# Streaming attention and a mixture of four experts on one core: a new order of the first loads, the second weight of expert 0 in two halves, and refitted constants of the planner

## The chip, the core and the metric

The kernel runs on one core of a Trainium2 chip. The metric is the device time of one execution in microseconds (us). The core has a matrix engine (TensorE, PE in the profile, with its weight loads as PEld), VectorE (DVE), ScalarE (ACT), GpSimd (POOL) and SyncE (SP), which run side by side and wait for each other by semaphores. Transfers go through DMA queues. POOL issues the loads that convert float32 to bfloat16. SP issues transposes, gates and stores.

## The reference

Inputs are q, k and v of shape (4, 8, 768, 64): batch, heads, positions, head dimension. A query sees the keys of the last 128 positions and the first 4 positions ("sinks"). The attention output is laid out as 3072 rows of 512 and goes through four experts, whose results are summed with weights:

```python
keep = is_sink | in_window                     # n_sink 4, window 128
a = softmax(where(keep, q @ k.T / 8, -1e9))
x = (a @ v).transpose(0, 2, 1, 3).reshape(3072, 512)
p = domain_probs / (domain_probs.sum(-1, keepdims=True) + 1e-09)
for e in range(4):
    h = np.maximum(x @ w1[e], 0.0)             # w1[e]: 512 x 1024
    out += p[:, e:e + 1] * (h @ w2[e])         # w2[e]: 1024 x 512
```

The output is float32, 3072 x 512.

## The kernel before

The whole program is unrolled. While it is emitted, a **planner** in the kernel file keeps a clock for each engine (`t["pe"]`, `t["act"]`, `t["dve"]`, `t["pool"]`, `t["sp"]`, and `t["sw"]` for the queue of POOL's loads) and adds a cost for each instruction that it emits. These clocks exist only while the program is made: on the chip each engine runs its instructions in the order in which they were emitted, and waits where a semaphore says so. So every constant of the planner acts on the program only through the order of the instructions, and through which buffer an instruction uses.

**Units of work.** A batch has three groups of 256 rows, here called pairs: (batch, pair). A *unit* is (batch, pair, expert): the hidden block `H` of 256 rows by 1024. It is made in one of three ways.

- Plain: products `hps` of 128x256 (L1134), for the units ahead of `START`.
- Fast: seven products in place of eight, on forms of w1 and of x that VectorE adds beforehand (L1224).
- Turning: the same seven products, P1 to P7, with 512 columns each, two matmuls to a product (L1336). Their result has rows and columns exchanged. It is gated into two row buffers (tiles `row0`, `row1`, later also `rest` and others) on ScalarE or VectorE, and two DMA transposes on SP (`H<-row`, L1317) bring it into `H`. `TURNED_UNITS` says which units are of this kind, 26 before.

In a turning unit the partial result of P5 is copied into the second row buffer by ScalarE (L1390), VectorE adds the bank of P1 and P6 to it, and P7 and P3 go on from that sum:

```python
def keep(engine):                       # after P5
    nc.scalar.copy(out=c5, in_=y)       # c5: the second row buffer as float32
    u["both"](act(n))
def both(ready):
    def run(engine):
        nc.vector.tensor_add(tiles["V"], c5, tiles["X"])
        at["P7"] = at["P3"] = dve(n)
```

A unit of this kind may be opened when two row buffers will be free soon; a transpose puts its buffer back with the time at which it is planned to be done:

```python
def halves(self):
    return sum(x[0] <= t["pe"] + REST for x in self.resting)
```

**Second products.** For the first two pairs the products with w2 are plain: `second` (L1597), eight matmuls of 512 columns for an expert and 128 rows into one bank `acc`. For the rest they are seven products of 256 columns on forms (`product`, L1511), after VectorE has made sums of `H` (L1451).

**Attention.** For each batch: q and k are loaded as rows (`qkn`, L267, key `n<block>` in the new list) and transposed, on TensorE for the first batch and by SP's DMA (`qkT<-qkn`, L276) later. Then come scores (`sps`, L720), exponentials on ScalarE, masks on VectorE, the product with v and the sinks (`od`, L783 and L790), a reciprocal and a scaling into `onat`, and a transpose into `xT`: on TensorE (`tx`, L854) or by SP's DMA (`xT<-onat`, L807).

**Loop.** At each step the planner lists what may come next on TensorE with the time at which it would be ready and a rank: an attention step, a step of an open unit or a new unit (`first`), a `second`, or a `product`. It emits the one of lowest rank that is ready. `DUE`, `LOW_SECOND`, `OPEN`, `STEP0`, `LOW_PRODUCT` and `HIGH_PRODUCT` are ranks. `SHARE_OF`, `LEAD`, `MIX`, `OVER`, `ALONE`, `BEHIND`, `HOLDS`, `SOON` and `REST` are thresholds. `GATE`, `GATE0`, `SCALED`, `FORM` and `TOKEN` are slacks, by which work for the other engines may be put off. Where nothing is ready in the first 20 us, products without a use (`idle_products`, L596) keep TensorE at work.

**Loads.** The rows of batch 0, w1 of expert 0 in quarters (L349), w2 of expert 0 (L359) and then the other weights are issued by POOL in a list written out by hand. `lands` estimates when each has landed. From the third batch on, a small copy on POOL (`held`, L212) stands in front of each load of q, k and v: it reads a tile that was written lately, so that the load is not issued before.

Of the kernel before, what the change touches and what calls it, by code (L numbers as in the profile page):

```python
# [16 lines left out]
def kernel(  # L17
# [20 lines left out]
    P = 128  # L38
# [24 lines left out]
    TURNED_UNITS = (0, 0, 0, 0, 1, 0, 0, 1, 0, 1, 0, 0, 0, 1, 1, 1, 1, 1, 1, 1, 1, 1, 1, 1, 1, 1, 1, 1, 1, 1, 1, 1, 1, 1, 1, 1)  # L63
    EXPERTS = {(1, 0): (0, 1, 2, 3), (1, 1): (2, 0, 3, 1), (1, 2): (1, 2, 3, 0), (2, 2): (0, 1, 3, 2), (3, 1): (3, 1, 0, 2), (3, 2): (1, 0, 3, 2), (2, 0): (1, 3, 0, 2), (0, 2): (2, 1, 3, 0), (3, 0): (2, 3, 0, 1), (2, 1): (3, 0, 1, 2), (0, 1): (2, 1, 3, 0)}
# [29 lines left out]
    SPACE = 1000  # L94
    GATE_LANDS = 2500
    WIDE = 2
    OPEN = 1.9
    SOON = 35000
# [7 lines left out]
    HOLDS = 3  # L106
# [3 lines left out]
    OVER = 6  # L110
    ALONE = 2.4
    BEHIND = 3900
# [10 lines left out]
    t = {"pe": 1200.0, "act": 0.0, "dve": 0.0, "pool": 1280.0, "sp": 800.0, "sw": 6500.0, "hw": 0.0}  # L123
# [87 lines left out]
    def hold():  # L211
        nc.gpsimd.tensor_copy(out=held, in_=mark[1])  # L212
        pool(2, mark[0])
    ROW = {64: 12.8, 128: 22.6, 256: 41.7, 512: 79.8, 1024: 156.2}
# [142 lines left out]
    def load_w2(e):  # L357
        w2_sb[e] = wpool.tile([P, NFB, Dout], BF16, name=f"w2_{e}", tag=f"w2_{e}")
        nc.gpsimd.dma_start(out=w2_sb[e], in_=moe_w2[e].rearrange("(fb p) d -> p fb d", p=P))  # L359
        lands(("w2", e), F, Dout)  # L360
# [163 lines left out]
    t["sw"] += 500  # L524
    for tb in (2, 3):
        load_nat(0, tb)
    load_v(0, (2, 3))
    load_w1(0, 4, [0])
    load_w1(0, 4, [1])
    load_w1(0, 4, [2])  # L530
    load_w1(0, 4, [3])
# [1291 lines left out]
```

## Time and profile before

| what | value |
|---|---|
| median of 3 runs | 353.14 us (352.71 to 353.69) |
| profiled execution | 352.58 us |
| its span | 350.9 us |
| mean granted clock of TensorE | 0.999 |
| TensorE busy | 345.4 us, 3470 matmuls |
| VectorE busy | 275.8 us |
| ScalarE busy | 215.3 us |
| GpSimd busy | 79.8 us |
| moved by DMA | 47.95 MB, mean 137 GB/s |

The span runs from the first to the last recorded instruction of the profiled execution, and the execution's own time is 1.7 us longer. The runs without profile differ by up to 1.0 us. Matmuls are pipelined, and their ends in the profile are modelled, so that the busy time counts overlaps; the distance from one start to the next tells what a matmul takes. In a timeline a row gives start, duration, engine, line, operation, tiles and count, and in brackets how long the engine was idle ahead of it and what released it. In a list of waits a row gives who waited at which line, for whom, the sum, the count and the longest.

### The profile page before, as it was taken

To read this page: it belongs to the slowest core of one execution; us is meant where nothing else is said; L and a number is where in the kernel's file an instruction comes from. 1 tells how busy PE (TensorE), PEld (TensorE's weight loads), DVE (VectorE), ACT (ScalarE), POOL (GpSimd) and SP (SyncE) were. 2 spreads that over 40 slices of the span, in tenths; PEclk is the share of its full clock that TensorE was granted. 3 is DMA by queue.
4 is the path that set the end of the run, shared out by engine and by line. 5 is a ranking of instruction groups with operands and counts; after the bars stand their busy time and mean duration, and the time that the engine had idled before them with its cause. 6 is when DMAs were issued, how large, how long until landed. Compare 5 with 4: busy or idle time off the path is not lost.

```text
span 350.9 us, 8955 instructions
## 1 busy us (share of the span) xinstructions
PE 345.4 (98%) x3470; PEld 256.2 (73%) x3470; DVE 275.8 (79%) x661; ACT 215.3 (61%) x491; POOL 79.8 (23%) x125
## 2 busy tenths in 40 slices
PE   8999999999999999999999999999999999999996
PEld 4685769756798988786997756856856666666785
DVE  5893999988999998899599779579769594785740
ACT  4865714437656576658545589389588666757411
POOL 8946114430542550800244100000000000000000
PEclk9999999999999999999999999999999999999999
DMA  9999999999996999995799976437336829244421
GB/s 177 178 187 194 220 206 173 176 161 160 172 113 78 167 165 164 158 115 64 99 152 183 141 141 146 91 91 138 73 102 140 153 60 182 60 113 128 92 91 62
DMA packets 173606, 47.95 MB, mean 137 GB/s; under 512 B 158084, under 2 KB 169572, under 8 KB 173564
## 3 DMA queue, kind: packets, MB, share of 16 engines
q0 software_dynamic: 79104, 17.31, 56.7%
q1 hardware_dynamic: 93404, 29.55, 44.8%
q8 instruction: 27, 0.44, 0.5%
q10 hardware_dynamic: 1056, 0.52, 0.5%
q14 instruction: 15, 0.12, 0.1%
HBM read 37.61 MB, written 6.34 MB: 125 GB/s over the span
## 4 chain that ended last, share of the span: by engine, by line
PE 94%; DVE 3%; DMA 1%; ACT 1%; issue 1%; DVEq 0%; ACTq 0%
PE acc L1511 34%; PE cps L1336 22%; PE cps L1224 12%; PE acc L1597 8%; PE hps L1134 7%; PE sps L720 3%; PE od L790 3%; PE acc L596 2%; DMA H<-row 1%; PE od L783 1%; DVE aT L758 1%; PE tx L854 1%; DVE onat L820 0%; PE tr L617 0%; PE sinks L681 0%
## 5 line engine op out<-in xcount | busy, mean ns | idle before, releaser
L1511 PEld LDWEIGHTS <-H 128*128 128x128 bf16 x708 | 66.4, 98 | 20.7 <-issue 1.9
L1511 PE MATMUL acc<-w,H 128*128 128x256 bf16 x420 | 57.4, 273 | 0.0
L748 ACT ACTIVATE aT<-sps 128x512 bf16<-128x512 f32 (+1 forms) x96 | 47.0, 573 | 5.4 <-PE sps L720 5.1
L1354 ACT ACTIVATE cps<-cps 128x512 f32<-128x512 f32 x51 | 29.6, 587 | 20.5 <-PE cps L1336 19.6
L1511 PEld LDWEIGHTS <-S 128*128 128x128 bf16 x320 | 30.6, 98 | 9.4 <-issue 0.6
L1134 PE MATMUL hps<-xT,w 128*128 128x256 bf16 x256 | 32.1, 273 | 0.1
L1336 PE MATMUL cps<-w,T 128*128 128x512 bf16 x104 | 30.9, 379 | 0.3 <-DVE cps L1384 0.3
L835 ACT ACTIVATE onat<-od,R 128x64 bf16<-128x64 f32 x108 | 25.0, 325 | 10.1 <-DVE R L817 9.9
L1336 PE MATMUL cps<-vf,T 128*128 128x512 bf16 x104 | 30.6, 379 | 0.0
L1336 PE MATMUL cps<-w,xT 128*128 128x512 bf16 x104 | 30.3, 379 | 0.0
L1597 PE MATMUL acc<-w,H 128*128 128x512 bf16 x128 | 29.9, 379 | 0.0
L1224 PEld LDWEIGHTS <-w 128*128 128x128 bf16 x448 | 28.2, 98 | 2.1
L1511 PE MATMUL acc<-wf,H 128*128 128x256 bf16 (+1 forms) x216 | 29.7, 271 | 0.0
L1336 PEld LDWEIGHTS <-T 128*128 128x128 bf16 x208 | 19.6, 98 | 11.1 <-issue 0.8
L1377 ACT COPY cps<-cps 128x512 f32<-128x512 f32 x26 | 15.0, 578 | 20.6 <-PE cps L1336 18.7
L1134 PEld LDWEIGHTS <-w 128*128 128x128 bf16 x256 | 24.1, 98 | 4.3 <-issue 0.5
L1572 ACT COPY osb<-acc 128x256 f32<-128x256 f32 x35 | 13.4, 382 | 21.3 <-PE acc L1511 19.9
L740 DVE TENSOR_TENSOR aT<-aT,masks 128x1024 bf16<-128x1024 bf16 (+1 forms) x36 | 22.7, 640 | 3.1 <-ACT aT L748 2.8
L336 POOL DMA_DIRECT2D vx<-in_v_dram x24 | 21.4, 897 | 16.2 <-PE acc L1597 4.8
L1257 DVE SCALAR_TENSOR_TENSOR H<-cps,gates 128x512 bf16<-128x512 f32 x36 | 24.0, 677 | 0.2 <-DMA gates<-gate_rows 0.2
L267 POOL DMA_DIRECT2D qkn<-in_q_dram x22 | 19.4, 882 | 13.5 <-DMA qkT<-qkn 5.4
L267 POOL DMA_DIRECT2D qkn<-in_k_dram x22 | 20.0, 911 | 7.7 <-DMA w<-in_moe_w_dram 6.6
(154 smaller groups left out, 696.7 us busy)
## 6 DMA issues: line engine op xcount, KB each, us to landing
w<-in_moe_w_dram POOLq DMA_DIRECT2D x6, 1024.0 KB, 18.2
out_dram<-osb SPq DMA_DIRECT2D x17, 256.0 KB
vx<-in_v_dram POOLq DMA_DIRECT2D x24, 128.0 KB, 5.8
qkn<-in_q_dram POOLq DMA_DIRECT2D x22, 128.0 KB, 7.3
qkn<-in_k_dram POOLq DMA_DIRECT2D x22, 128.0 KB, 7.2
gates<-gate_rows SPq DMA_DIRECT2D x14, 128.0 KB
w<-in_moe_w_dram POOLq DMA_DIRECT2D x4, 256.0 KB, 6.7
w<-in_moe_w_dram POOLq DMA_DIRECT2D x2, 512.0 KB, 11.7
```

The costliest lines, as they stand in the source:

```text
L267: nc.gpsimd.dma_start(out=nat[b, tb][:, i], in_=(q, k)[i][b, :, tb * P:(tb + 1) * P, :].rearrange("h p d -> p h d"),)
L336: nc.gpsimd.dma_start(out=vx[tb][:, :, 0:D], in_=v[b, :, tb * P:(tb + 1) * P, :].rearrange("h p d -> p h d"),)
L740: nc.vector.tensor_mul(x, x, m[:, None, :].to_broadcast([P, 2 if g == 0 else 4, w if g == 0 else 2 * P]))
L748: nc.scalar.activation(out=a[:, ph], in_=sps[ph][:, 0:w], func=AF.Exp, scale=scale)
L835: nc.scalar.mul(o[:, qi, hp, ph * D:(ph + 1) * D], od[:, qi, ph, 0:D], R[:, qi, ph])
L1134: nc.tensor.matmul(h[:, i].rearrange("p (q n) -> p q n", q=2), lhsT=w1_sb[e][:, db, fb * P:(fb + 1) * P], rhs=xT[b, g][:, :, db], start=(i ...
L1224: nc.tensor.matmul(y[:, f], lhsT=A[:, d, f * P:(f + 1) * P], rhs=T[:, d], start=(m in ("P1", "P5") and f == 0 and d == 0), stop=(d == 1), ...
L1257: nc.vector.scalar_tensor_tensor(out=dst, in0=src, scalar=0.0, in1=gate, op0=ALU.max, op1=ALU.mult)
L1336: nc.tensor.matmul(y.rearrange("p f n -> p (f n)"), lhsT=T[:, d], rhs=A[:, d], start=(m in ("P1", "P5") and d == 0), stop=(d == 1), skip_g ...
L1354: nc.scalar.activation(out=src, in_=src, func=AF.Relu)
L1511: nc.tensor.matmul(y, lhsT=self.operand(b, g, e, m)[:, f], rhs=forms[e][m][:, f, cs], start=(k == 0 and f == 0 and m in (("P1", "P5", "P2" ...
L1597: nc.tensor.matmul(op, lhsT=H[:, fb // QF, fb % QF, s], rhs=w2_sb[e][:, fb, :], start=(fb == 0), stop=(fb == NFB - 1),)
```

## The change

1. The first loads are issued in an order that is given as a list. Before: n2 n3 v2 v3, the four quarters a0 to a3 of w1 of expert 0, then its whole w2, n4 n5 v4 v5, the halves b0 b1 of w1 of expert 1, w2 of expert 1, w1 and w2 of expert 2. After: n2 v2 n3 v3 a0 to a3 s0, then n4 s1 v5 n5 b0 v4 b1 t1 c t2, where s0 and s1 are the halves of w2 of expert 0, t1 and t2 the w2 of experts 1 and 2, and c is w1 of expert 2.
2. The second products of expert 0 are split in the same way: for a pair the first four matmuls of both 128-row blocks, each into a bank of its own, and the last four of both as two further steps.
3. The estimates of when loads land are refitted (`LANDED`, `LATER`, `ROW[256]`, the start of `t["sw"]`).
4. Most other constants of the planner have new values, with the order of experts for each pair (`EXPERTS`) and the choice of turning units (27 in place of 26) among them.
5. Values need both of their v blocks by the estimates; `held` copies one float32 where it copied two bfloat16; idle products are not emitted while both banks are taken; weight forms may be made from a planned 41 us on (`SOON2`).

Which units are plain and which of seven products (`START`) is as before. In the order of instructions of the changed kernel, the matmuls are those of before, except that 56 of 128 columns become 14 of 512, one of 512 columns is added to fill a bank that was never written, three idle products of 256 columns are missing, and there are three more runs of score products between others.

```diff
-    TURNED_UNITS = (0, 0, 0, 0, 1, 0, 0, 1, 0, 1, 0, 0, 0, 1, ...)
+    TURNED_UNITS = (0, 0, 1, 0, 0, 1, 0, 1, 0, 1, 0, 0, 1, 1, 1, 1, 1, 1, 0, 1, ...)
-    EXPERTS = {(1, 0): (0, 1, 2, 3), (1, 1): (2, 0, 3, 1), ...
+    EXPERTS = {(1, 0): (1, 3, 2, 0), (1, 1): (1, 0, 3, 2), ...
-    MIX = 9
-    SHARE_OF = (1.1, 0.94, 0.98)
-    LEAD = (0.995, 0.985)
-    DUE = 2.0
+    MIX = 4
+    SHARE_OF = (1.07, 0.94, 0.96)
+    LEAD = (1.03, 0.94)
+    DUE = 1.2
-    LOW_SECOND = 2.4
-    HIGH_PRODUCT = 2.0
+    LOW_SECOND = 3.2
+    HIGH_PRODUCT = 1.8
-    GATE = 700
-    GATE0 = 1200
-    FORM = 2500
-    TOKEN = 4250
-    MARGIN = 2400
+    GATE = 100
+    GATE0 = 1100
+    FORM = 7000
+    TOKEN = 4000
+    MARGIN = 2700
-    STEP0 = 0.16
+    STEP0 = 0.3
-    REST = 1500
+    REST = 5000
-    SCALED = 1500
+    SCALED = 500
+    LANDED = 1100
+    W2PARTS = 2
+    ORDER = ('n2', 'v2', 'n3', 'v3', 'a0', 'a1', 'a2', 'a3', 's0', 'n4', 's1', 'v5', 'n5', 'b0', 'v4', 'b1', 't1', 'c', 't2')
+    HEAD = 10
+    SOON2 = 41000
+    LATER = {("w2", 1): 800, ("w1", 2): 850, ("w2", 2): 700, ("w1", 1, 0): 300}
-    OPEN = 1.9
-    SOON = 35000
+    OPEN = 1.6
+    SOON = 22000
-    HOLDS = 3
+    HOLDS = 1
-    OVER = 6
-    ALONE = 2.4
-    BEHIND = 3900
+    OVER = 2
+    ALONE = 2.3
+    BEHIND = 4200
...
-    t = {..., "sw": 6500.0, ...}
+    t = {..., "sw": 5700.0, ...}
...
-        nc.gpsimd.tensor_copy(out=held, in_=mark[1])
+        nc.gpsimd.tensor_copy(out=held.bitcast(FP32), in_=mark[1].bitcast(FP32))
...
+        t["sw"] += LATER.get(key, LATER.get(key[:2], 0.0))
         at = max(t["sw"], issued + 800)
         t["sw"] = at + rows * ROW[cols] / 16
-        landed[key] = t["sw"] + 900
+        landed[key] = t["sw"] + LANDED
...
-    def load_w2(e):
-        w2_sb[e] = wpool.tile([P, NFB, Dout], BF16, name=f"w2_{e}", tag=f"w2_{e}")
-        nc.gpsimd.dma_start(out=w2_sb[e], in_=moe_w2[e].rearrange("(fb p) d -> p fb d", p=P))
-        lands(("w2", e), F, Dout)
+    def load_w2(e, parts=1, which=None):
+        ...
+        for i in which or range(parts):
+            nc.gpsimd.dma_start(
+                out=w2_sb[e][:, i * n:(i + 1) * n],
+                in_=moe_w2[e][i * n * P:(i + 1) * n * P].rearrange("(fb p) d -> p fb d", p=P),
+            )
+            lands(("w2", e, i) if i < parts - 1 else ("w2", e), F // parts, Dout)
...
-            ((weight_form, e) for e in range(E) if ahead and form_due(e)), None)
+            ((weight_form, e) for e in range(E) if (ahead or t["pe"] > SOON2) and form_due(e)), None)
...
-    for tb in (2, 3):
-        load_nat(0, tb)
-    load_v(0, (2, 3))
-    load_w1(0, 4, [0])
     ...
-    load_w2(0)
+    for i in ORDER[:HEAD]:
+        items[i][0](*items[i][1:])
...
-                    self.second += [(g, s, e) for s in range(2)]
+                    n = W2PARTS if e == 0 else 1
+                    self.second += [(g, s, e, i, n) for i in range(n) for s in range(2)]
...
-            for fb in range(NFB):
+            for fb in range(i * NFB // n, (i + 1) * NFB // n):
...
-        if soonest < 20000 and soonest > now + 220:
+        if soonest < 20000 and soonest > now + 220 and min(acc_free) < 1e11:
             idle_products(acc[1], 1, G)
```

More of the change, by code (lines that the diff above doesn't have):

```diff
@@ L1580, in second_ready @@
                 return 1e12
-            g, s, e = self.second[0]
-            return max(acc_free[self.turn % 2], landed.get(("w2", e), 1e12), self.H_at.get((0, g, e), 1e12))
+            g, s, e, i, n = self.second[0]
+            free = 0.0 if i else acc_free[self.turn % 2]
+            return max(free, landed.get(("w2", e, i) if i < n - 1 else ("w2", e), 1e12), self.H_at.get((0, g, e), 1e12))
         def emit_second(self):
             ready = self.second_ready()
-            g, s, e = self.second.pop(0)
+            g, s, e, i, n = self.second.pop(0)
             if g not in out_sb:
@@ L1600, in emit_second @@
                 )
-            end = pe(NFB * Dout, ready, n=NFB)
+            end = pe(NFB * Dout // n, ready, n=NFB // n)
             acc_free[bank] = 1e12
+            self.done += NFB * Dout // n
+            self.since = 0
+            if i < n - 1:
+                return
             sc = scale_t[:, 2 * g + s, e:e + 1]
@@ L1618, in emit_second @@
             later("dve" if e else "act", end, 400, run)
-            self.since = 0
-            self.done += NFB * Dout
             if s == 1:
@@ L1658 @@
     asked = []
[L1659 to L1661 removed]
+    loads, turns = [items[i] for i in ORDER[HEAD:]], []
     def nat_loads(b, tbs):
```

40 lines of the change are left out of this document (20 added, 20 removed).

## Prediction

> **What bounds the kernel now.** I read the page first, for the span, the engines' busy time and the chain that ended last.
>
> ```profile
> span 350.9 us, 8955 instructions
> PE 345.4 (98%) x3470; PEld 256.2 (73%) x3470; DVE 275.8 (79%) x661; ACT 215.3 (61%) x491; POOL 79.8 (23%) x125
> PE 94%; DVE 3%; DMA 1%; ACT 1%; issue 1%; DVEq 0%; ACTq 0%
> ```
>
> TensorE is busy in 98% of the span and is 94% of the chain. So the time is TensorE's work at its own rate, and a change of order can only remove or add holes between products. Next I read the waits of TensorE, which list the holes, and a table by stretches of time, to see whether the middle has room left (columns: stretch, us, then PE, PEld, DVE, ACT and POOL busy with counts, granted clock, DMA share, GB/s).
>
> ```profile
> PE acc L596 <- DVE lent L506: 1.4, 1, 1.4
> PE cps L1336 <- DVE cps L1384: 0.3, 1, 0.3
> PE tx L854 <- DVE onat L820: 0.2, 1, 0.2
> ...
> 175.00:200.00 25.00, 25.00 (x314) 21.19 (x312) 23.34 (x56) 12.52 (x37) 8.80 (x15) 1.00 1.47 164
> ```
>
> After the start there is one named hole of 0.3 us and one of 0.2 us. In the middle TensorE is full. There is little left to gain, and any new hole shows at its full length. The one hole is the most useful place of the trace, so I read its timeline.
>
> ```profile
> 156.50 0.59 PE L1336 MATMUL cps<-w,xT 128*128 128x512 bf16 x2
> 156.93 0.59 PE L1336 MATMUL cps<-vf,T 128*128 128x512 bf16 x2
> 157.36 0.60 PE L1511 MATMUL acc<-w,H 128*128 128x256 bf16 x4
> 157.79 0.59 PE L1336 MATMUL cps<-vf,T 128*128 128x512 bf16 x2
> ...
> 159.02 0.60 PE L1511 MATMUL acc<-w,H 128*128 128x256 bf16 x4
> 159.91 0.59 PE L1336 MATMUL cps<-w,T 128*128 128x512 bf16 x2 [0.29 <-DVE cps L1384]
> 160.34 0.59 PE L1336 MATMUL cps<-vf,xT 128*128 128x512 bf16 x2
> 160.86 0.40 PE L720 MATMUL sps<-qkT 64*128 64x128 bf16 x6
> 161.19 0.61 PE L1511 MATMUL acc<-w,H 128*128 128x256 bf16 x4
> ```
>
> Starts give the prices, since the modelled ends overlap. Two products of 512 columns take 0.43 us (156.50 to 156.93), four of 256 take 0.43 us (157.36 to 157.79, 0.109 each), and 128 columns take 0.055. At 159.02 four products of 256 columns should have ended at 159.46, and the next starts at 159.91: the hole costs 0.45 us. Entering a run of scores costs 0.09 us more than its products (160.34 to 160.86 is 0.52 for two of 512).
>
> ```profile
> 154.62 1.79 SPq L1317 DMA_TRANSPOSE H<-row  x1
> 158.54 0.59 ACT L1390 COPY row<-cps 128x512 f32<-128x512 f32 x1 [0.84 <-DMA H<-row]
> 159.16 0.70 DVE L1384 TENSOR_TENSOR cps<-row,cps 128x512 f32<-128x512 f32 x1 [0.72 <-ACT row L1390]
> ```
>
> This is why it is there. A turning unit (seven products P1 to P7 that leave a transposed hidden block in two `row` buffers) copies its P5 result into a row buffer on ScalarE, VectorE adds it, and P7 needs the sum. ScalarE waited 0.84 us because the transpose that empties this buffer for the unit before, issued at 154.62, had not landed until 158.54: 3.92 us from issue to release. From the copy's start to P7's start are 1.37 us.
>
> **The row buffers (REST 1500 to 5000).** REST is how far ahead of a buffer's planned release a turning unit may be opened. In the changed program's order one unit is opened much sooner behind its predecessor than any now: batch 2, pair 0, expert 3 takes both row buffers right after expert 0 of that pair. Its ScalarE copy to `row0` (L1399, once L1390) waits for the transpose of `row0` that ends a run of five on SP: q/k block 4 of batch 3, attention output, q/k block 5, `row1`, `row0`. SP issues them in order, and the attention output is ready only after a reciprocal and four ScalarE scalings.
>
> ```profile
> 160.63 0.18 DVE L817 RECIPROCAL R<-od 128x4 f32<-128x4 f32 x1
> 160.84 0.93 ACT L835 ACTIVATE onat<-od,R 128x64 bf16<-128x64 f32 x4 [0.24 <-DVE R L817]
> ...
> 184.18 9.03 SPq L276 DMA_TRANSPOSE qkT<-qkn  x3
> 193.30 1.26 SPq L807 DMA_TRANSPOSE xT<-onat  x1
> 194.65 2.81 SPq L1317 DMA_TRANSPOSE H<-row  x2
> ...
> 219.36 1.26 SPq L1317 DMA_TRANSPOSE H<-rest  x1
> 222.33 0.37 ACT L1572 COPY osb<-acc 128x256 f32<-128x256 f32 x1 [1.38 <-DMA H<-rest]
> ```
>
> I count from the last attention-output product. Reciprocal and scalings take 1.14 us (160.63 to 161.77), with the hand-over from TensorE some 1.4. Three issues on SP follow before that of `row0` (output, q/k, `row1`), at 1.35 each (193.30 to 194.65): 4.0. From issue to release I have 2.97 us (219.36 to 222.33) and 3.92 us (above). Then 1.37 to P7. In all 9.7 to 10.7 us. The changed order gives TensorE in that time 4 score products (0.22), P4 (0.43), sixteen of 256 (1.74), 8 score products (0.44), eight of 256 (0.87), P1 and P5 (0.87), eight of 256 (0.87), P6 and P2 (0.87), eight of 256 (0.87): 7.2, with two entries into scores 7.4. The rest, 2.3 to 3.3 us, is a hole in front of P7: nothing behind it on TensorE may pass. SP's q/k transpose can itself wait for its rows: the three from 184.18 took 9.03 where three at 1.35 take 4.05, so 1.7 each more, which would make up to 5. If it misses everything, or the transposes are issued sooner than I count, it is nothing. I take 3.6: the middle of 2.3 to 3.3, and half of 1.7. P3 and P4 queue behind P7, and the two row transposes of this unit come as much later; their reader, the second products of that pair, lies several us behind.
>
> **The first loads and the halves of w2.** In front of the first w2 the same rows and w1 quarters stand in POOL's queue as before, only n3 and v2 change places, so its start there is unchanged.
>
> ```profile
> 9.51 3.00 POOL L349 DMA_DIRECT2D w<-in_moe_w_dram  x4
> 12.44 0.95 POOL L359 DMA_DIRECT2D w<-in_moe_w_dram  x1
> ...
> w<-in_moe_w_dram POOLq DMA_DIRECT2D x1, 1024.0 KB, 12.7
> w<-in_moe_w_dram POOLq DMA_DIRECT2D x1, 256.0 KB, 7.9
> ...
> 21.73 3.87 PE L1134 MATMUL hps<-xT,w 128*128 128x256 bf16 x32
> 25.43 5.34 PE L1597 MATMUL acc<-w,H 128*128 128x512 bf16 x24
> ```
>
> The whole w2 of expert 0 is issued at 12.44 and lands 12.7 later, at 25.1. The last w1 quarter is issued 3/4 into the run of four that ended at 12.44, at 11.7, and lands at 19.6. So w2 has the queue for 5.5 us and its first half would land at 19.6 + 2.8 = 22.4. The first product of w2 stood at 25.43, where 32 products from 21.73 end at 25.22: a wait of 0.2, which goes. In the changed order it stands 32 products (3.5), three idle ones (0.33) and two small transposes (0.1) sooner: 21.5. It then waits 0.9 for the first half, and no idle products are planned for it. Net +0.7; at the least −0.2 (it lands sooner than half of it), at the most +2 if n4, which now stands between the halves, delays the second.
>
> The Trainium skill, page "DMA: Bandwidth & Descriptors", section "Anatomy of one DMA — SWDGE (gpsimd) path", gives a DMA of GpSimd's queue a fixed part of about 2.0 us beside its bytes, mostly in the completion, which speaks against halves: by it alone, and if transfers did not overlap, the sum would be 2 us higher. The row of w2 (5.5 us behind four quarters that are themselves queued) leaves no 2 us per transfer on top of the bytes, so I add none.
>
> **Small terms.** 27 units turn in place of 26: 56 products of 128 columns become 14 of 512, the same columns, −0.1. One of the turned units needs a filler of 512 columns: +0.22. Three runs of scores more: +0.27. Three idle products of 256 fewer: −0.33. The hole of 159.91 need not come back: −0.45. Weight forms start earlier on VectorE (FORM, SOON2); I cost that at nothing because they stand where VectorE has slack, 79% busy; in 175 to 200 it has only 1.7 of 25 us, and what falls there would come through in part.
>
> **Sum.** 3.6 + 0.7 − 0.1 + 0.22 + 0.27 − 0.33 − 0.45 = +3.9. The profiled execution took 352.58 us, its span and 1.7 around it; the median of the runs is 353.14, 0.56 above. So 356.5 for a profiled run and **357.0** for the median. About 0.3%, 1.06 us, is what a measurement here can tell from no change.
>
> **Rivals.** *The row buffer is empty in time* (same). If SP reaches the five transposes 3 us before I count, because q/k rows are in early, the 3.6 goes and the sum is +0.3: 353.4. For it: the hole of 159.91 was only 0.45 long. Against: the transpose of the attention output follows products that TensorE itself has only just made, so it can't be early, and `row1` and `row0` stand behind it. Chance 0.08.
>
> *Early gaps close and no row wait comes* (faster). In the first stretch small waits stand between short runs, where v2 in front of n3 may help:
>
> ```profile
> 8.20 0.39 PE L617 MATMUL tr<-ident,qkn 128*128 128x128 bf16 x4
> 8.70 0.34 PE L790 MATMUL od<-vx,aT 128*128 128x65 bf16 x6
> ...
> 14.67 0.66 PE L720 MATMUL sps<-qkT 64*128 64x128 bf16 x6
> 15.26 0.39 PE L596 MATMUL acc<-lent 128*128 128x256 bf16 x2
> ```
>
> Four of 128 columns take 0.22, and 0.50 pass: 0.28. Six take 0.33, and 0.59 pass: 0.26. With the 0.2 of the wait for `onat` in the first list, and the small terms (−0.4), it is −1.1: 352.0. It decides only if the row wait and the w2 wait are both below 0.3. Chance 0.14.
>
> *POOL holds the row buffers* (slower still). In the changed order POOL's `held` copies, which only mark time between loads, read a row buffer six times, once before, so that the next writer of it waits for POOL.
>
> ```profile
> POOL held L1726 <- DMA qkT<-qkn: 28.4, 2, 15.7
> ```
>
> POOL stands in such waits, 28.4 us in two of them, and a held copy behind a q/k pair of loads waits for two issues of 0.95 (as at 12.44). One such writer on TensorE's path: +1.9, 358.9. It decides if the load behind which POOL waits is later than the row's transposes. Chance 0.08.
>
> *The clock falls in the hole* (slower still). The rows below show that products right after the idle start run slowly.
>
> ```profile
> 1.41 4.66 PE L596 MATMUL acc<-lent 128*128 128x512 bf16 x13 [1.41 <-DVE lent L506]
> 5.91 0.61 PE L617 MATMUL tr<-ident,qkn 128*128 128x128 bf16 x8
> ```
>
> Thirteen of 512 columns took 4.50 us where thirteen at 0.216 take 2.8: 1.7 lost. If a hole of over 3 us does the same again, the sum is +5.6: 358.7. Against it: no hole of the trace of before is that long, so it shows neither. Chance 0.06. The Trainium skill, page "TensorE: Matmul & The Clock Gate", section "HAM oscillation — how this bites in real kernels", warns of idle gaps over about 3.4 us, after which the clock is halved until some 3.4 us of work are done. The slow start agrees with it; by its rule a hole of 3.6 would pay, but the window runs free and mostly splits such a hole.
>
> **Numbers.** Forecast 0.64 (355.3 to 358.8 with the bounds of the row wait), same 0.08, faster 0.14, POOL 0.08, clock 0.06. Slower is 0.64 + 0.08 + 0.06 = 0.78. The range goes from the middle of the faster case, 351.9, to 359.6, above the two dear ones: some 0.07 are left out below it and as many above, where the row wait has 5 us or two prices add.
>
> **What would show it.** In the changed profile the waits of TensorE must have a line for P7 (cps, released by VectorE's sum) of 2 to 5 us near 190, with ScalarE's copy to `row` waiting for the transpose of `row` before it, and SP's five transposes in front; a line of up to 1 us at the first product of w2 near 22; idle products 14 and 9. Wrong if TensorE's longest hole after 45 us is under 1 us, if SP's `row0` transpose lands before the copy is asked, or if the span falls while the waits stay. If clock is lost, products after the hole are 0.43 us apart for 512 columns.

## The result and the profile after

| | before | after |
|---|---|---|
| median | 352.92 us (4 runs) | 373.38 us (371.04 to 374.36, 4 runs) |
| ratio | | 1.0567, 95% interval 1.0514 to 1.0621 |
| profiled execution | 352.58 us | 373.63 us |
| mean granted clock of TensorE | 0.999 | 0.982 |

The change makes the kernel 5.7% slower, 20.5 us, where 4 were forecast. The page of the changed kernel, with the lines that answer to those of before:

```profile
span 371.9 us, 8866 instructions
PE 352.2 (95%) x3426; PEld 255.9 (69%) x3426; DVE 275.2 (74%) x656; ACT 222.0 (60%) x493; POOL 80.7 (22%) x126
PE 75%; DMA 9%; DVE 7%; POOL 4%; ACT 2%; issue 2%; SPq 1%; POOLq 0%; DVEq 0%; ACTq 0%
```

TensorE's share of the chain falls from 94% to 75%; transfers take 9% and VectorE 7%. The waits of TensorE say where:

```profile
PE cps L1345 <- DVE cps L1393: 9.5, 4, 4.7
PE acc L1520 <- DMA H<-row: 2.7, 1, 2.7
PE acc L603 <- DVE lent L519: 1.4, 1, 1.4
PE hps L1143 <- ACT aT L755: 1.2, 2, 0.7
```

The first line is the kind that was 0.3 us in one hole before: P7 of a turning unit behind VectorE's sum. Now it is 9.5 us in four holes. The fourth line is new too: in the first 20 us TensorE waits twice for ScalarE's exponentials. To see what else there is, I took the distance from each product's start to the next and subtracted the median distance of the same shape in the profile of before. What is left over is 10.5 us before and 31.2 after. Of these 20.7 us more, 1.1 fall in the first 20 us of work, 0.9 in the stretch of 80 to 100, 8.4 in that of 120 to 160, 7.7 in that of 180 to 200 and 2.4 in that of 260 to 280 (counted in work done, so that equal places stand beside each other).

The longest hole is the one that was forecast, in batch 2, pair 0, expert 3. The timeline, all engines:

```profile
197.07 1.93 SPq L814 DMA_TRANSPOSE xT<-onat  x1
199.24 1.51 SPq L283 DMA_TRANSPOSE qkT<-qkn  x1
200.84 4.03 SPq L1326 DMA_TRANSPOSE H<-row  x2
202.26 1.04 PE L1520 MATMUL acc<-w,S 128*128 128x256 bf16 x8
206.59 0.59 ACT L1399 COPY row<-cps 128x512 f32<-128x512 f32 x1 [5.67 <-DMA H<-row]
207.21 0.69 DVE L1393 TENSOR_TENSOR cps<-row,cps 128x512 f32<-128x512 f32 x1 [4.81 <-ACT row L1399]
207.95 1.01 PE L1345 MATMUL cps<-w,T 128*128 128x512 bf16 x2 [4.66 <-DVE cps L1393]
208.76 1.06 PE L1345 MATMUL cps<-vf,xT 128*128 128x512 bf16 x2
209.61 1.91 PE L1520 MATMUL acc<-w,S 128*128 128x256 bf16 x8
211.32 1.06 PE L1345 MATMUL cps<-w,T 128*128 128x512 bf16 x2
```

Eight products from 202.26 end at 203.13, P7 starts at 207.95: 4.82 us. ScalarE stood 5.67 us in front of its copy until SP's transposes had emptied the row buffer; the last of them, the second of the two from 200.84, was issued at 203.61. And the products behind the hole are slow: two of 512 columns take 0.81 and 0.85 us instead of 0.43, eight of 256 take 1.71 instead of 0.87. The table by stretches (granted clock in the third column from the right) shows why:

```profile
202.00:208.00 6.00, 1.34 (x11) 0.93 (x10) 1.09 (x2) 1.38 (x4) 0.00 (x0) 0.86 0.91 136
208.00:213.00 5.00, 5.00 (x18) 2.64 (x18) 2.52 (x5) 2.30 (x4) 0.00 (x0) 0.50 0.13 30
```

From 208 to 213 the clock is at half. That costs 2.3 us more. The second place, near 132, has two waits in a row and then the same half clock (0.54 from 135 to 142):

```profile
120.91 6.48 SPq L283 DMA_TRANSPOSE qkT<-qkn  x2
127.51 5.72 SPq L1326 DMA_TRANSPOSE H<-row  x2
131.69 0.60 PE L1520 MATMUL acc<-w,H 128*128 128x256 bf16 x4
133.68 0.19 POOL L1738 COPY held<-qkT 128x2 bf16<-128x2 bf16 x1 [10.63 <-DMA qkT<-qkn]
135.00 1.89 PE L1520 MATMUL acc<-w,H 128*128 128x256 bf16 x8 [2.70 <-DMA H<-row]
135.86 0.59 ACT L1399 COPY row<-cps 128x512 f32<-128x512 f32 x1 [6.03 <-POOL held L218]
137.22 1.01 PE L1345 MATMUL cps<-w,T 128*128 128x512 bf16 x2 [0.34 <-DVE cps L1393]
```

Here SP has two q/k transposes ahead of the row transposes, and the second of them waited 3.7 us for its rows. The row transposes are issued at 127.51 and 132.00, and the first product that reads them starts only at 135.00. Behind it, ScalarE's copy had waited for a `held` copy of GpSimd that reads the row buffer, and that one for the same q/k transposes. The holes lose 2.87 and 0.65 us, the half clock 2.4. Two shorter holes follow, of the kind of the first and of a new one:

```profile
162.49 1.24 SPq L1326 DMA_TRANSPOSE H<-row  x1
168.16 0.59 ACT L1399 COPY row<-cps 128x512 f32<-128x512 f32 x1 [4.13 <-DMA H<-row]
169.53 0.59 PE L1345 MATMUL cps<-w,T 128*128 128x512 bf16 x2 [2.26 <-DVE cps L1393]
...
303.20 0.43 DVE L1460 TENSOR_TENSOR S<-qkT 128x512 bf16<-128x512 bf16 x1 [2.45 <-DMA qkT<-row]
306.00 0.69 DVE L1393 TENSOR_TENSOR cps<-rest,cps 128x512 f32<-128x512 f32 x1
306.74 0.59 PE L1345 MATMUL cps<-w,T 128*128 128x512 bf16 x2 [2.20 <-DVE cps L1393]
```

At 167 a row transpose took 5.7 us from issue (162.49) to the copy that it releases (168.16). At 303 VectorE itself stood in front of a sum of transposed `H` for 2.45 us, with the sum for P7 behind it in its queue. These two lose 2.42 and 2.37.

The semaphores in the trace tell when each transfer landed, and they show why a row transpose is late. SP's transfers land in the order of their issue, in all of the 126 neighbouring pairs whose landings can be told. Most row transposes of the changed kernel land 2.8 us after their issue, but a q/k transpose takes 7.2 us (median of 18, at the most 12.3), so what is issued soon behind one lands late. Near 132 the q/k transpose of 126.16 landed at 133.56 and the first row transpose, issued at 127.51, at 134.95. Near 167 the row transpose of 162.49 landed at 168.08, behind a load of gates that was issued at 161.92 and landed at 167.17. In the kernel before it is the same (2.8 us, and 6.5 with 11.7 at the most for q/k), so this was to be seen ahead of the change.

### The profile page after: what moved, and what is told of

It reads as the page before. It is cut to its first block, busy times and chain, and to the rows that moved or that the text cites. A ratio compares the mean times of both kernels' runs of the same rounds, so it can differ in the third digit from the quotient of the medians.

```text
span 371.9 us, 8866 instructions
## 1 busy us (share of the span) xinstructions
PE 352.2 (95%) x3426; PEld 255.9 (69%) x3426; DVE 275.2 (74%) x656; ACT 222.0 (60%) x493; POOL 80.7 (22%) x126
## 4 chain that ended last, share of the span: by engine, by line
PE 75%; DMA 9%; DVE 7%; POOL 4%; ACT 2%; issue 2%; SPq 1%; POOLq 0%; DVEq 0%; ACTq 0%
PE acc L1520 29%; PE cps L1345 18%; PE cps L1233 9%; PE acc L1609 7%; PE hps L1143 6%; DMA H<-row 3%; DMA w<-in_moe_w_dram 3%; PE sps L727 3%; PE od L797 2%; DMA qkT<-row 2%; POOL qkn L274 1%; DVE H L1266 1%; POOL vx L343 1%; DVE row L1370 1%; DMA H<-rest 1%
## 5 line engine op out<-in xcount | busy, mean ns | idle before, releaser
L1520 PEld LDWEIGHTS <-H 128*128 128x128 bf16 x732 | 69.7, 99 | 26.8 <-issue 3.2
L1520 PE MATMUL acc<-w,H 128*128 128x256 bf16 x432 | 59.2, 277 | 2.8 <-DMA H<-row 2.7
L1363 ACT ACTIVATE cps<-cps 128x512 f32<-128x512 f32 x57 | 33.3, 588 | 22.3 <-PE cps L1345 22.0
L1345 PE MATMUL cps<-w,T 128*128 128x512 bf16 x108 | 33.7, 397 | 9.5 <-DVE cps L1393 9.5
L1345 PE MATMUL cps<-w,xT 128*128 128x512 bf16 x108 | 32.1, 379 | 0.0
L1520 PE MATMUL acc<-wf,H 128*128 128x256 bf16 (+1 forms) x224 | 31.0, 271 | 0.0
L842 ACT ACTIVATE onat<-od,R 128x64 bf16<-128x64 f32 x96 | 22.5, 334 | 12.0 <-DVE R L824 9.9
L1143 PEld LDWEIGHTS <-w 128*128 128x128 bf16 x256 | 24.1, 98 | 5.9 <-DMA w<-in_moe_w_dram 1.7
L1233 PEld LDWEIGHTS <-w 128*128 128x128 bf16 x416 | 25.7, 98 | 2.9 <-issue 0.3
L1386 ACT COPY cps<-cps 128x512 f32<-128x512 f32 x27 | 15.7, 581 | 11.7 <-PE cps L1345 11.6
L1266 DVE SCALAR_TENSOR_TENSOR H<-cps,gates 128x512 bf16<-128x512 f32 x33 | 22.3, 683 | 0.2
L1460 DVE TENSOR_TENSOR S<-H 128x512 bf16<-128x512 bf16 x36 | 14.8, 418 | 10.1 <-PE acc L1520 5.0
```

The source lines that it names most:

```text
L842: nc.scalar.mul(o[:, qi, hp, ph * D:(ph + 1) * D], od[:, qi, ph, 0:D], R[:, qi, ph])
L1143: nc.tensor.matmul(h[:, i].rearrange("p (q n) -> p q n", q=2), lhsT=w1_sb[e][:, db, fb * P:(fb + 1) * P], rhs=xT[b, g][:, :, db], start=(i ...
L1233: nc.tensor.matmul(y[:, f], lhsT=A[:, d, f * P:(f + 1) * P], rhs=T[:, d], start=(m in ("P1", "P5") and f == 0 and d == 0), stop=(d == 1), ...
L1266: nc.vector.scalar_tensor_tensor(out=dst, in0=src, scalar=0.0, in1=gate, op0=ALU.max, op1=ALU.mult)
L1345: nc.tensor.matmul(y.rearrange("p f n -> p (f n)"), lhsT=T[:, d], rhs=A[:, d], start=(m in ("P1", "P5") and d == 0), stop=(d == 1), skip_g ...
L1363: nc.scalar.activation(out=src, in_=src, func=AF.Relu)
```

## The experiments

All were run beside the kernel before, whose medians were 352.7 to 353.1 us.

**Theory A: row buffers, and the clock after them.** *c5_in_H*: the partial result of P5 goes into the unit's own hidden block.

```diff
-            c5 = X[1].rearrange("p f t n -> p (f t n)")...
+            c5 = H[:, 1].rearrange("p f t n -> p (f t n)")...
```

> The changed kernel in the same order on every engine; only the partial result of P5 is kept in the unit's own, still empty hidden block instead of in its second row buffer, so that the copy of P5 no longer waits for the readers of that row buffer. Theory A (row buffers taken over too early, and the clock falls after the long hole): the holes in front of P7 near 137, 167 and 203 us (0.6, 2.3 and 4.7) go, and the slow products after the last one with them (2.3 us); the hole near 132 (2.7, a product waiting for transposed H) and its slow clock stay: 373.4 - 7.6 - 2.3 = about 363.5. Rival B (the transposes themselves are late, and with the copy free the next step waits for them as long): above 370.

363.99 us (ratio 1.0301, 1.0254 to 1.0348), the time that theory A gave: 9.4 us of the 20.5 go with this one dependence and what follows it. That the sum fits so well is partly luck. The half clock near 132, which was to stay (2.4 us), is not in this profile (1.00 from 130 to 140), waits of 0.9 and 0.7 us in front of P7 are left near 136 and 167, and near 203 there is a new hole:

```profile
201.73 1.47 PE L1520 MATMUL acc<-wf,H 128*128 128x256 bf16 x12
203.07 0.69 ACT L1366 ACTIVATE row<-cps,own_gates 128x512 bf16<-128x512 f32 x1 [3.98 <-DMA H<-row]
204.92 0.36 ACT L1581 COPY osb<-acc 128x256 f32<-128x256 f32 x1
205.34 3.51 PE L1520 MATMUL acc<-w,H 128*128 128x256 bf16 x16 [2.14 <-ACT osb L1581]
```

ScalarE now waits 3.98 us at the next writer of the row buffer, and the copy that empties a bank of TensorE stands behind it in its queue: 2.14 us, after which sixteen products take 3.35 us, 0.21 each: the half clock again.

*hold_no_rows*: GpSimd's `held` copies off the row buffers.

```diff
-                    marked(at, X[k][:, 0, s, 0:2])
+                    mark[0] = at
```

> The changed kernel in the same order; only the small copies on GpSimd that stand in front of loads no longer read row buffers (they read the last other tile that was marked). Rival C (GpSimd, which waits in one of these copies for the q/k transposes, holds the row buffer): the hole in front of P7 near 137 goes, and if the hole near 132 comes from the same cause, its 2.7 us and the slow clock after it (2.4) too: 367.5. Theory A: only the 0.6 us at 137 go, since P7 stood behind the wait for H anyway, and the slow clock follows from the 2.7 us alone: 372.5 to 373.4.

372.13 us (1.0549, 1.0514 to 1.0584). The waits of TensorE:

```profile
PE cps L1345 <- DVE cps L1393: 10.3, 4, 6.0
PE acc L1520 <- DMA H<-row: 3.2, 1, 3.2
```

Rival C falls: the hole near 132 stays (3.2), and four holes in front of P7 too, the 0.6 us near 137 among them that theory A gave up. In the changed kernel GpSimd held the buffer until 135.79, but SP's transpose of it landed only at 135.76.

*after_rest1500* and *before_rest5000*: only REST exchanged.

```diff
-    REST = 5000
+    REST = 1500
```

> The changed kernel with one constant put back, REST 1500; the planner then makes another order. Theory A: no turning unit opens more than a planned 1.5 us ahead of its buffers, so holes of 2 us and more in front of P7 released by the copy of P5 are gone; some 7 us of holes and 2 of slow clock less, 362 to 366. Rival D (the holes come from the other constants, the slacks and ranks): as many holes, 370 or more.

366.09 us (1.038, 1.0344 to 1.0415): 7.3 less than the changed kernel, 0.1 above theory A's range. A hole of 2.4 is left near 132, and near 167 one of 2.0 in front of P7, of the kind that theory A had gone.

> The kernel before with one constant changed, REST 5000; the planner makes another order. Theory A: holes in front of P7 behind a copy that waits for a transpose appear, 2 to 5 us each, with slow products after those over 3 us: 357 to 366. Rival D: within 2 us of the kernel before, 352 to 355.

354.56 us (1.0039, 1.0026 to 1.0052), below theory A's range. Its waits:

```profile
PE cps L1336 <- DVE cps L1384: 1.8, 1, 1.8
```

The hole that was 0.3 near 158 is 1.8. So REST by itself opens one hole of the right kind, and a small one; among the other new constants the same number goes with 7.3 us.

*filled_hole*: useless products where TensorE waits near 203.

```diff
+    FILL = {(2, 0, 3): 18}
...
+            if m == "P7" and (b, g, e) in FILL:
+                i = next(i for i in range(6) if ring[i] <= t["pe"])
+                x = bank(i, [P, 2 * G], FP32, "fill")
+                for _ in range(FILL[b, g, e]):
+                    nc.tensor.matmul(x, lhsT=A[:, 0][:, 0:P], rhs=A[:, 0], start=True, stop=True)
```

> The changed kernel in the same order, with 18 products without a use (512 columns, 3.9 us) put into a free bank in front of P7 where the hole of 4.7 us near 203 stands; they work while TensorE would wait. Theory A (the clock falls because TensorE stood idle for over 3 us): the hole shrinks to about 1 us, the products behind it are 0.216 us apart from the first, and 2.3 us are gained: 371. Rival J (the slow products come from something else, such as weights or data that arrive slowly): products behind the hole still 0.43 apart, 373.4 or, with the fillers in the way, more.

369.82 us (1.0489, 1.0465 to 1.0512). The timeline of TensorE, and the stretch behind the hole:

```profile
202.75 4.05 PE L1349 MATMUL fill<-w 128*128 128x512 bf16 x18
207.72 0.59 PE L1351 MATMUL cps<-w,T 128*128 128x512 bf16 x2 [0.92 <-DVE cps L1399]
208.15 0.59 PE L1351 MATMUL cps<-vf,xT 128*128 128x512 bf16 x2
208.58 1.04 PE L1526 MATMUL acc<-w,S 128*128 128x256 bf16 x8
```
```profile
207.00:212.00 5.00, 4.28 (x34) 3.26 (x34) 3.80 (x8) 2.92 (x6) 0.00 (x0) 1.00 0.15 35
```

P7 starts as late as in the changed kernel, at 207.72, but two products of 512 take 0.43 at once and the clock is 1.00: the slow products behind this hole come from the idle time. With more work the kernel is 3.6 us faster than the changed one, where 2.3 were expected. Not all of that is the filler's: in this profile the hole near 304 is gone too (2.4 us), and the clock is at half from 168.4 to 171.9, behind the hole near 167, where it was not in the changed kernel.

**Theory H: SP's order.** *rows_first_c5*: c5_in_H and hold_no_rows together, and one q/k transpose behind the row transposes on SP.

```diff
+        if (b, tb) == (2, NQB - 1):
+            behind_rows.extend([2, start])   # started after the next two H<-row
```

> As c5_in_H (363.99), with the small copies on GpSimd off the row buffers, and on SP one q/k transpose (block 5 of batch 2) moved behind the two row transposes that follow it; TensorE's order is the same. Theory H (the hole at 132 is there because the row transposes stand on SP behind a q/k transpose that itself waits 3.7 us for its rows): the holes of 2.2 and 1.1 us near 132 and 136 and the slow products between them go, about 4 us: 359 to 361. Rival I (the transposes are late there in any order because loads fill the queues): 363 to 365.

365.05 us (1.0355, 1.0312 to 1.0398): no gain over c5_in_H. Near 132 the product's wait for `H` falls from 2.0 to 0.6 us, and P7's behind it grows from 0.9 to 1.5. TensorE's waits have a new line, at 147:

```profile
PE acc L1532 <- DVE osb L1582: 2.5, 1, 2.5
```

*after_turn_late*: q/k transposes planned 3 us later.

```diff
-        ... landed.get(("qk", *turns[0]), 1e12) < now and ...
+        ... landed.get(("qk", *turns[0]), 1e12) < now - (3000 if turns[0][0] > 1 else 0) and ...
```

> The changed kernel with q/k transposes of batches 2 and 3 put on SP only a planned 3 us after their rows land. Theory K: the transpose that waited 3.7 us for its rows in front of the row transposes no longer does, the hole near 132 (2.7 us, 0.6 at P7, 2.4 of slow products) goes and the holes near 167, 203 and 304 stay: 366 to 369. Rival I (transposes are late there in any order because loads fill the queues): 371 to 374.

371.55 us (1.0523, 1.0472 to 1.0574), within the spread of the changed kernel:

```profile
PE cps L1345 <- DVE cps L1393: 10.9, 4, 5.6
```

The product's wait for `H` is gone, and P7 comes 3.1 us late near 132 instead. Rival I is nearer in time: one wait taken away there uncovers the next. Whether the loads are the cause, as it says, is not shown.

**The loads and the planner.** *loads_only* is the changed kernel with all old ranks, slacks and thresholds, units and experts (REST 1500, DUE 2.0, SHARE_OF 1.1 and so on), so that the loads, the halves, the landings and most of the small edits of point 5 are left of the change.

> The changed kernel with the planner's old ranks, slacks and thresholds, REST among them, and the old choice of units and experts; what is left of the change is the order of the first loads, the halves of w2 with the split products and the refitted landings. Theory E (the early part costs the wait for the first half of w2 and no more): 353 to 354.5, no hole over 1.5 us after 40 us. Rival F (the new loads bring TensorE ahead): 351 to 352.5. Rival G (any other order of loads sends the planner into holes as in the changed kernel): above 357.

362.74 us (1.0277, 1.0254 to 1.03), as rival G had it. The largest hole, in the timeline:

```profile
132.71 2.63 SPq L283 DMA_TRANSPOSE qkT<-qkn  x1
135.44 0.52 SPq L509 DMA_DIRECT2D gates<-gate_rows  x1
137.28 0.69 DVE L1266 SCALAR_TENSOR_TENSOR H<-cps,gates 128x512 bf16<-128x512 f32 x1 [4.42 <-DMA gates<-gate_rows]
138.02 0.50 PE L727 MATMUL sps<-qkT 64*128 64x128 bf16 x4 [3.40 <-DVE H L1266]
```

No row buffer is in it: gates stand on SP behind a q/k transpose (SP waited 4.5 us for rows in two of these from 124 to 136), VectorE waits for the gates, TensorE for a bank.

*after_old_loads* is the other half, the changed kernel with the loads of before:

```diff
-    W2PARTS = 2
-    ORDER = ('n2', 'v2', 'n3', 'v3', 'a0', 'a1', 'a2', 'a3', 's0', 'n4', 's1', ...)
+    W2PARTS = 1
+    ORDER = ('n2', 'n3', 'v2', 'v3', 'a0', 'a1', 'a2', 'a3', 's0', 'n4', 'n5', ...)
```

> The changed kernel with the first loads in the old order and w2 of expert 0 whole; all other constants new. If the ranks, slacks and thresholds make the holes (theory A and D together): two or more holes of over 2 us behind transposes remain, 364 to 376. If the new loads make them (rival G): 353 to 358.

370.07 us (1.0487, 1.0434 to 1.0539): theories A and D. With the old loads the new constants still make holes of over 2 us behind transposes, one near 139 and one near 301. In both VectorE stood in front of a sum of transposed `H`, as near 304 in the changed kernel. The longer one:

```profile
PE sps L727 <- DVE H L1266: 4.3, 1, 4.3
```

*landings_only* and *order_only* split loads_only. The first is the kernel before with the new estimates, the second is loads_only with the old ones:

```diff
-        landed[key] = t["sw"] + 900
+        landed[key] = t["sw"] + 1100
...                                  # and ROW[256] and the additions of LATER
```

> The kernel before with only the estimates of landings changed (LANDED, ROW for 256 columns, the additions of LATER); loads, w2 and all other constants as before. The planner makes another order from early on. Theory K (the planner counts on transposes and gates too early where a q/k transpose on SP waits for its rows; only an order fitted to the chip avoids holes near 130 us, and any newly made one has them): a hole of 2 to 5 us between 125 and 145 us, 356 to 364. Rival L (the order of loads or the halves make the hole of loads_only): 352 to 354.5.

359.24 us (1.0188, 1.0167 to 1.0209): theory K's time, but not its hole; the longest single loss is 0.8 us, and the 6 us are scattered.

> The kernel before with the new order of the first loads and w2 of expert 0 in halves, with the old estimates of landings and all old constants. Theory K: again a hole between 125 and 145 us behind SP, 356 to 364. Rival M (the refitted landings make the hole of loads_only): 352 to 354.5.

360.29 us (1.021, 1.0168 to 1.0253). Again theory K's time without its hole: between 125 and 145 the longest loss is 1.0, and the largest wait stands near 87, has no releaser in the profile, and is not explained:

```profile
PE sinks L688 <- issue: 2.7, 1, 2.7
```

Two edits that each cost 6 to 7 us and together 10 do not look like a price of loads. *before_share* was to test that, but the kernel that ran had another constant, TOKEN 4000 for 4250 and SHARE_OF as it was, and with it TensorE's order of before:

> The kernel before with one number changed, the first of SHARE_OF from 1.1 to 1.07 (one of the new values): attention of the second batch is spread over less of the other work. Nothing of loads, landings or row buffers is touched; the order differs from the middle of the first batch on. Theory K: a hole near 130 us too, or one elsewhere behind SP, 354.5 to 362. Rivals L and M: 352 to 354.

353.14 us (1.0003, 0.999 to 1.0015): it says only that this constant does nothing. Three further kernels test it.

*pinned_halves*: the halves of w2, the second behind q/k block 4, in before's order of everything else, with the planner's sums untouched.

```diff
+            if e == 0:
+                half_w2(0)
...                                  # and half_w2(1) behind load_nat(0, 4)
```

> The kernel before with w2 of expert 0 loaded in two halves, the second behind q/k block 4; the planner's bookkeeping and with it the order of all other instructions on every engine is that of before. Theory N (the loads themselves cost little; the 6 to 10 us of loads_only, landings_only and order_only come from the order that the planner makes anew): 352.9 to 353.8, with at most 0.5 us of wait at the first products of w2. Rival O (the halves themselves are dear, each with a fixed part, and delay what stands behind them): 355 or more.

353.35 us (1.0011, 1.0000 to 1.0023, 12 runs): theory N. The halves themselves cost 0.6 us at the most: the interval begins at 1.0000. The profile has 0.5 us more lost in the first 20 us than before's, but that of before_c5 below, which loads as before, has as much.

*b_share107* and *b_due12*: before with one number changed.

```diff
-    SHARE_OF = (1.1, 0.94, 0.98)
+    SHARE_OF = (1.07, 0.94, 0.98)     # b_due12: DUE = 1.2
```

> The kernel before with the first number of SHARE_OF 1.07 instead of 1.1, nothing else; the planner's order differs from about a quarter of TensorE's products on. Theory N in its strong form (any order made anew has holes near SP's transposes): 355 to 362, holes between 100 and 230 us. Weak form (only some do): 352.5 to 354.5.

366.66 us (1.0393, 1.0373 to 1.0413), slower than the strong form said, with a hole of 7.4 us in the timeline:

```profile
196.69 1.88 SPq L807 DMA_TRANSPOSE xT<-onat  x1
205.22 1.24 SPq L276 DMA_TRANSPOSE qkT<-qkn  x1
...
210.14 2.02 SPq L1317 DMA_TRANSPOSE H<-gates  x1
216.56 1.04 PE L1511 MATMUL acc<-w,H 128*128 128x256 bf16 x4 [7.28 <-DMA H<-gates]
```

In front of the q/k transpose of 205.22 SP stood 6.6 us for its rows. That wait alone does not explain the hole: ScalarE finished the row buffer that TensorE's product needed (here `gates`) only at 209.02, and SP issued its transpose at 210.14. By the semaphores it landed at 216.51, 6.4 us after its issue, behind a q/k transpose that was issued at 207.23 and landed at 215.48.

> The kernel before with DUE 1.2 instead of 2.0, nothing else; a second new order, different from the first tenth of TensorE's products on. Strong form of theory N: 355 to 362. Weak form: 352.5 to 354.5.

356.1 us (1.0088, 1.0072 to 1.0103): the strong form, at its lower edge, with no loss over 0.61 in one place.

**What makes a new order dear.** *after_lands* and *share_lands* change the planner's estimate of when a row transpose lands.

```diff
-    LANDS = -1400
+    LANDS = 1600
```

> The changed kernel with one number of the planner changed, LANDS from -1400 to 1600: row transposes count as landed 3 us later, for the readers of H and for the row buffers alike. Theory P (the holes are there because the planner counts on transposes too early): the holes behind H<-row and behind the copies of P5 shrink below 1 us, and with the slow products gone 357 to 365. Rival Q (each new order just exchanges its holes for others, because q/k transposes, gates and GpSimd's copies are miscounted as well): 366 to 376.

363.42 us (1.0297, 1.0258 to 1.0336), in theory P's range of time: 10 us less by one number. The waits:

```profile
PE cps L1345 <- DVE cps L1393: 3.4, 3, 3.0
```

Holes near 167, 203 and 304 are gone; one of 3.0 near 132 stays, behind a copy of P5 that waited 4.33 us for a row transpose, so theory P holds in part.

> b_share107 (366.66) with LANDS 1600 instead of -1400. Theory P: the hole of 7.4 us near 209 goes, 353 to 358. Rival Q: a hole of 2 us or more in another place, 358 to 368.

360.65 us (1.0216, 1.0199 to 1.0233), rival Q's time without its hole. The largest line of TensorE's waits after the start:

```profile
PE acc L1511 <- ACT acc L1550: 0.8, 2, 0.6
```

The 7.4 us went, and 6 us were gained. Nearly 8 over before remain in losses of under 0.8 us; what makes these was not found. The profiled run has a half clock from 162.4 to 165.8, but the other three runs (360.4 to 360.7 us) had a mean clock of 1.000.

*before_c5*: the edit of c5_in_H in the kernel before.

> The kernel before in its own order with the partial result of P5 kept in the unit's empty hidden block, as in c5_in_H. Theory A: the one hole in front of P7 (0.45 us at 159.9) goes and nothing takes its place: 352.5, a gain of 0.1%, at the edge of what can be told. Rival B (the next writer of the row buffer waits as long): 352.9, or slower where ScalarE then stands in that wait with other work behind it, up to 354.

353.29 us (1.0014, 1.0001 to 1.0027): rival B's time, but its mechanism is not seen: ScalarE, the next writer of the row buffer, goes on to it at 160.11 without a wait. The wait in front of P7 is no longer in the list, and the time is not better. No version was found that beats the kernel before.

## Why the prediction was wrong

**The step that failed** is the one from the new order to the sum. The sum had the first loads at +0.7 and one place in which something waits for SP at +3.6; the rest of the new order it took as counts of instructions, −0.4 together. So it put all other places at nothing, without a reason. The runs showed 7.1 us in that one place, with the clock behind the hole, and in three more near 132, 167 and 304 another 5.9, 2.4 and 2.4: 10.7 us where the sum had nothing.

**The row wait** was right in mechanism and in its unit, and too small: 3.6 us were given, 4.82 measured. The chain behind it (SP's five transposes, ScalarE's copy, VectorE's sum, P7) is there as described, and nearly every term came as counted. From the last attention-output product to SP's issue it took 1.4 us (195.7 to 197.07), from the issue of `row0` to the copy 2.98 (203.61 to 206.59), from there to P7 1.36, and TensorE had 7.4 us of work. The term that was too small is the three issues ahead of `row0`: 6.5 us (197.07 to 203.61) where three at 1.35, 4.0, were counted. And "one unit is opened much sooner behind its predecessor" is not all: the copy of P5 waits in three places, near 136, 167 and 203, not in one. c5_in_H put that dependence with its consequences at 9.4 us.

**The clock** was a rival at 1.7 us with 0.06. It came twice, at 2.4 and 2.3. The price was about right; the argument against it ("no hole of the trace of before is that long") said nothing of the changed kernel, for which the sum itself had a hole of over 3 us. filled_hole shows the cause. The Trainium skill, page "TensorE: Matmul & The Clock Gate", section "HAM oscillation — how this bites in real kernels", has the rule of the prediction, no idle gaps over about 3.4 us; by it the rival deserved far more beside that hole. The hole near 132, with 2.7 us without work, is shorter than that rule has it and paid too.

**The first loads** were given +0.7, and 1.1 us more are lost in the first 20 us of work. That these are near each other is luck. The first half of w2 landed at 22.27, as counted (22.4), but TensorE came to it only at 22.32 and not at 21.5, so the wait of 0.9 did not come (c5_in_H and hold_no_rows, with the same order, have 0.3 and 0.2). What came is the two waits for ScalarE's exponentials, 1.2 us, which the sum did not have. Right is that halves do not cost a fixed 2 us each: in pinned_halves the two halves and the two loads of n4 have all landed at 26.82, and in the kernel before w2 and the same two loads at 26.81. The fixed part of about 2.0 us that the Trainium skill, page "DMA: Bandwidth & Descriptors", section "Anatomy of one DMA — SWDGE (gpsimd) path", gives for each DMA is not added once more here.

**The small terms** (+0.22, +0.27, −0.33, −0.45 and −0.1) are counts, and a new order is not just its counts. In twelve kernels the planner made an order anew from changed constants, loads or estimates: the changed kernel, after_rest1500, before_rest5000, loads_only, after_old_loads, landings_only, order_only, b_share107, b_due12, after_lands, share_lands and after_turn_late. Each is slower than before, by 1.5 to 20 us. The edits with before's order (pinned_halves, before_share, before_c5) cost 0.2 to 0.6. How the constants of before were found is not on record, so it stays open whether a new order is dear as such or before's is an unusually good one.

**The bounds** of the forecast, 355.3 to 358.8, do not follow from its own row wait of 2.3 to 5 us, which gives 355.7 to 358.4; the result lies far above both.

**POOL holding the row buffers** did happen (6.03 us of ScalarE near 136), with little weight: hold_no_rows moved the time by 1.3 us, within the spread of the runs.

**Shown and open.** Shown: the row-buffer dependence (c5_in_H), the clock after the hole near 203 (filled_hole), the small price of the loads themselves (pinned_halves), and that one planner constant without any load in it costs 14 us (b_share107). Supported, not shown: that the planner's estimate of landings is a part of the cause. after_lands and share_lands gain 10 and 6 us, but both start from bad orders, and from such an order another constant gained 7.3 (after_rest1500). Read from traces only: that q/k transposes hold up what is behind them on SP, by waiting for rows and by landing late; the two runs that tried to take the first away near 132 found the next wait in its place. Open: why each of these orders has the holes it has, and the scattered losses of landings_only, share_lands and b_due12.

## What to carry to other kernels

Where a program's order comes out of a planner with modelled times, a changed constant is a new program: before its local terms are summed, its order has to be searched for every place where a copy, a sum or a product stands behind a transfer, and each such place priced with what stands ahead of it in its queue, not by the usual landing of its own kind. SP issued and landed its transfers in order here, so a transfer whose data is late, or which lands late itself (q/k transposes), puts that on what is behind it. When the sum contains a hole of over 3 us on TensorE, the half clock behind it belongs into the sum and not among the rivals: in these profiles it came after every one of more than 3.1 us.

## What the runs showed of the hardware

The granted clock falls after holes shorter than I had expected, and not after every one. In these profiles it fell to half after all seven holes of TensorE of more than 3.1 us: 3.16 and 5.97 (hold_no_rows), 3.40 (loads_only), 4.29 (after_old_loads), 4.66 (changed kernel), 5.55 (after_turn_late) and 7.28 (b_share107). Between 1.9 and 3.0 us it goes either way. It fell after 2.14 (c5_in_H, near 205), 2.19 and 2.32 (filled_hole), 2.21 (after_rest1500), 2.29 (after_old_loads), 2.70 (changed kernel, near 132) and 2.93 (after_turn_late). It stayed at 1.00 after 1.99 (c5_in_H, near 134), 2.20 and 2.26 (changed kernel, near 306 and 169), 2.22 (hold_no_rows), 2.55 (rows_first_c5), 2.69 (order_only) and 2.96 (after_lands, near 135).

A single hole is not needed. In share_lands the clock is 0.50 from 162.4 to 165.8, and no wait of TensorE in the 5 us ahead is longer than 0.3 us; it was busy in 70% of the stretch from 160 to 162.4. Each of these half clocks lasted 3.4 us (205.2 to 208.7 in c5_in_H) or 6.8 (206.3 to 213.1 in the changed kernel), and it can begin within the hole. It also differs between runs of one program: the four runs of the changed kernel go from a mean clock of 0.976 with 374.36 us to 0.991 with 371.04.

A row transpose took 2.8 us from issue to landing in most cases and up to 7.4 (127.51 to 134.95) in the same program, behind others on SP. The stretch of 110 to 135 us, where loads and transposes meet, has a DMA share of 1.6 before and 1.7 in the changed kernel.
